# Chunked attention and a snake MLP: PSUM tiles in three shared slots, first loads issued together, V rows in four DMAs

## The chip, the cores and the metric

The kernel runs on one core of one Trainium2 chip. The metric is the device time of one execution in microseconds (us). The kernel before has three timed runs: 314.2, 314.21 and 312.73 us, median 314.2.

## What is computed

Four batches of eight heads with 768 positions of 64 values go through attention in chunks of 32 queries; each chunk sees its own 32 keys, 16 before, 8 after, and 8 memory keys of its head. The result, 3072 rows of 512, goes through a two-layer MLP with a snake activation.

```python
# per chunk c (32 queries), all batches and heads
k_full = concat([mem_k, k[c_start-16 : c_end+8]]); v_full = the same of mem_v, v
a = softmax(0.125 * q_c @ k_full.T)
x[c] = a @ v_full                     # x as (3072, 512)
# MLP
h = x @ w_in                          # 512 -> 2048
g = h + sin(alpha * h)**2 / alpha
out = g @ w_out                       # 2048 -> 512, float32
```

## The kernel before, in words

The program is written in the order in which each engine executes it; nothing reorders it. Each engine runs its own list from front to back, and waits in that list for the others.

**Loads.** Every load but one small one is issued by POOL: q and k of batch 0 in pairs of heads (L93), the memory keys and values (L145, L148), V of a batch in 16 DMAs (`load_v`, L116 and L120, two for each of eight blocks), the first-layer weights in eight DMAs (L181), the second-layer weights in four (L187), q and k of later batches in one DMA each (L106). POOL also copies the memory values into the V tiles (`put_memv`, L127) and the memory keys into the transposed keys (`put_memk`, L134).

**Attention of a batch.** For a pair of heads, VectorE copies k or q side by side (`pair_up`, tile `pr`, L195), TensorE transposes it (`t_k` L203, `t_q` L218), and ScalarE and VectorE bring the transpose into `kTi` and `qz` (L204, L210, L219, L223). Then `burst` goes over eight blocks of 96 queries: scores on TensorE (`qk_exp`, tile `sc`, L233), three exponentials on ScalarE (L247), and some steps later (the lag) the product with V (`pv`, tile `ot`, L261), the division by the row sum on VectorE (L264, L265) and a transpose into `xT` (L275, L278).

**First layer of a batch** (`l1`, 16 tiles `ft` of 128 of the 2048 columns): eight matmuls into `hT` (L301), a sine on ScalarE into `u` (L308), its square on ScalarE (L313) or VectorE (L311), and on VectorE the sum into `gT` (L314), which reads `hT` a second time and so frees its slot.

**Second layer** (`l2`): 96 matmuls of 512 columns (L327), 16 for each of six row groups; then the group is copied out of PSUM (L335 on VectorE, L337 on ScalarE in turn) and stored. They are handed out piecemeal as a filler: some in each step of the next batch's burst (`shares`), two behind each tile of the next first layer, the rest in one piece behind that.

**PSUM.** The pool `big` holds two slots of two 512-wide float halves, used by `sc` and `hT`; `opp` holds one slot for `o`; `atp` holds three small slots for transposes and `ot`. A tile waits until the readers of the slot's last tile are done.

**Order of the whole:** transposes of batch 0, burst 0, first layer 0 (with the transposes of batch 1 between its tiles, each behind the `l1` of its tile), burst 1 with second layer 0 as filler, first layer 1, and so on; the second layer of batch 3 ends the program.

## Time and profile before

| | |
|---|---|
| median of three timed runs | 314.2 us |
| profiled execution | 310.93 us, span 309.2 us |
| TensorE (PE) busy | 228.8 us, 74% of the span |
| VectorE (DVE) busy | 169.6 us, 55% |
| ScalarE (ACT) busy | 169.9 us, 55% |
| GpSimd (POOL) busy | 92.5 us, 30% |
| granted TensorE clock, mean | 0.961 |

How to read it: the span runs from the first to the last instruction of the profiled execution; its time is 1.7 us longer. "Busy" adds up an engine's instructions; matmul durations include the pipeline's length, so back-to-back matmuls overlap in it. In the rows that follow, the number before "us" or "ns" is what one instruction or one group took, and what stands behind an arrow is what ended the idle time before it. The stages lie, by the first rows of each in the timeline, at 0 to 43 us (loads, transposes, burst 0), 43 to 92.4 (first layer 0), 92.4 to 119.5 (burst 1), 119.5 to 159.9 (first layer 1), 159.9 to 181.3 (burst 2), 181.3 to 221.7 (first layer 2 and the rest of second layer 1), 221.7 to 244.1 (burst 3), 244.1 to 279.6 (first layer 3), 279.6 to 309.2 (the rest of second layer 2, all of second layer 3).

### The profile page before, as it was taken

Reading aid. Unit: us, or ns where it says so; the run is one execution under the profiler, and the core shown is the slowest. Engines: PE = TensorE matmul, PEld = TensorE weight load, DVE = VectorE, ACT = ScalarE, POOL = GpSimd, SP = SyncE. Lnnn points to the kernel's source line nnn. Section 1 sums busy time; section 2 is a strip of 40 time slices with the busy share of each in tenths; the row PEclk is TensorE's granted clock in tenths of the full one; section 3 lists DMA queues with packets and bytes.
Section 4 is the critical chain, followed back from the end, with each engine's and each line's share of the span. In section 5 each row is a group of like instructions: output and inputs, shape, how many; then the busy total and the mean of one; then the engine's idle time right before and its main releaser. Section 6 shows DMA issues by size and latency. Waiting matters only on the chain.

```text
span 309.2 us, 4313 instructions
## 1 busy us (share of the span) xinstructions
PE 228.8 (74%) x1604; PEld 130.5 (42%) x1604; DVE 169.6 (55%) x358; ACT 169.9 (55%) x256; POOL 92.5 (30%) x163
## 2 busy tenths in 40 slices
PE   1443783566739987888859978998789878887994
PEld 1331641333524553445435534545355444443441
DVE  6441653298870573677766646777566365554000
ACT  2435525277666505778885637798566367761000
POOL 8629985127967900000164900000000000000000
PEclk9999959699986999999989999999999999999999
DMA  8904999999499710000199900000101000001111
GB/s 100 113 1 29 91 144 199 205 205 101 30 145 144 106 37 34 2 34 0 9 182 146 97 34 2 35 0 2 68 19 51 36 0 34 0 3 69 68 68 69
DMA packets 54165, 20.97 MB, mean 68 GB/s; under 512 B 36736, under 2 KB 51072, under 8 KB 54144
## 3 DMA queue, kind: packets, MB, share of 16 engines
q0 software_dynamic: 48624, 14.40, 44.1%
q1 hardware_dynamic: 5520, 6.30, 5.8%
q8 instruction: 12, 0.20, 0.3%
q14 instruction: 9, 0.07, 0.1%
HBM read 28.78 MB, written 6.29 MB: 113 GB/s over the span
## 4 chain that ended last, share of the span: by engine, by line
PE 43%; DVE 21%; ACT 18%; POOL 7%; issue 5%; DMA 4%; DVEq 0%; ACTq 0%
PE o L327 22%; PE hT L301 15%; ACT u L308 8%; DVE gT L314 8%; ACT s L313 5%; DMA k_bf<-in_k_dram 4%; DVE s L311 4%; PE sc L233 2%; DVE qz L223 2%; DVE o_sb L335 2%; POOL w_in_sb L181 2%; POOL vw L120 2%; PE tk L203 2%; PE ot L261 2%; ACT o_sb L337 2%
## 5 line engine op out<-in xcount | busy, mean ns | idle before, releaser
L301 PE MATMUL hT<-xT,w_in_sb 128*128 128x384 bf16 x512 | 95.4, 332 | 24.2 <-DVE gT L314 22.8
L327 PE MATMUL o<-w_out_sb,gT 128*128 128x512 bf16 x384 | 102.6, 387 | 10.7 <-DVE o_sb L335 6.8
L314 DVE SCALAR_TENSOR_TENSOR gT<-s,inv_alpha,hT 128x768 bf16<-128x768 f32 x64 | 64.8, 1013 | 44.0 <-ACT s L313 39.8
L308 ACT ACTIVATE u<-hT,alpha_sb 128x768 f32<-128x768 f32 x64 | 57.7, 901 | 50.2 <-PE hT L301 49.9
L301 PEld LDWEIGHTS <-w_in_sb 128*128 128x128 bf16 x512 | 50.5, 99 | 68.3 <-issue 36.6
L247 ACT ACTIVATE pt<-sc,biasm 128x256 bf16<-128x256 f32 x96 | 37.9, 477 | 29.4 <-PE sc L233 29.4
L327 PEld LDWEIGHTS <-gT 128*128 128x128 bf16 x384 | 35.4, 99 | 39.7 <-issue 15.1
L313 ACT ACTIVATE s<-u 128x768 f32<-128x768 f32 x44 | 37.1, 843 | 1.4
L265 DVE TENSOR_TENSOR x_blk<-ot,rinv 96x256 bf16<-96x256 f32 x64 | 26.9, 421 | 2.2
L264 DVE RECIPROCAL rinv<-ot 96x4 f32<-96x4 f32 x64 | 11.1, 173 | 29.9 <-PE ot L261 29.9
L120 POOL DMA_DIRECT2D vw<-in_v_dram x32 | 23.3, 728 | 13.6 <-DMA q_bf<-in_q_dram 9.0
L337 ACT COPY o_sb<-o 128x512 f32<-128x512 f32 x12 | 7.0, 583 | 34.8 <-PE o L327 34.8
L233 PE MATMUL sc<-qz,kTi 128*128 128x192 bf16 x128 | 18.9, 283 | 8.9 <-DVE qz L223 6.0
L203 PE MATMUL tk<-ident,pr 128*128 128x128 bf16 x96 | 9.6, 248 | 21.3 <-DVE pr L195 21.3
L116 POOL DMA_DIRECT2D vw<-in_v_dram x32 | 22.0, 687 | 7.9 <-DMA w_out_sb<-in_moe_w_out_dram 4.2
L311 DVE TENSOR_TENSOR s<-u 128x768 f32<-128x768 f32 x20 | 19.2, 958 | 6.3 <-ACT u L308 6.0
L261 PE MATMUL ot<-vw,pt 128*128 128x65 bf16 x256 | 15.7, 203 | 9.1 <-DMA vw<-in_v_dram 3.9
L335 DVE COPY o_sb<-o 128x512 f32<-128x512 f32 x12 | 8.2, 687 | 25.8 <-PE o L327 25.8
L204 ACT COPY kTi<-tk 128x672 bf16<-128x672 bf16 x16 | 11.3, 707 | 18.2 <-PE tk L203 18.2
L261 PEld LDWEIGHTS <-pt 128*128 128x128 bf16 x256 | 13.1, 103 | 18.5 <-issue 4.0
L127 POOL COPY vw<-memv_st 8x512 bf16<-8x512 bf16 x32 | 18.9, 635 | 0.1
L233 PEld LDWEIGHTS <-kTi 128*128 128x128 bf16 x128 | 12.4, 111 | 12.6 <-issue 8.4
(43 smaller groups left out, 146.8 us busy)
## 6 DMA issues: line engine op xcount, KB each, us to landing
out_dram<-o_sb SPq DMA_DIRECT2D x24, 256.0 KB, 2.0
k_bf<-in_k_dram POOLq DMA_DIRECT2D x3, 768.0 KB, 8.6
q_bf<-in_q_dram POOLq DMA_DIRECT2D x3, 768.0 KB, 9.5
w_in_sb<-in_moe_w_in_dram POOLq DMA_DIRECT2D x8, 256.0 KB, 8.0
w_out_sb<-in_moe_w_out_dram POOLq DMA_DIRECT2D x4, 512.0 KB, 19.1
vw<-in_v_dram POOLq DMA_DIRECT2D x28, 64.0 KB, 3.5
vw<-in_v_dram POOLq DMA_DIRECT2D x28, 56.0 KB, 3.4
k_bf<-in_k_dram POOLq DMA_DIRECT2D x4, 192.0 KB, 4.0
```

The costliest lines, as they stand in the source:

```text
L116: nc.gpsimd.dma_start(vw[r0:64, :, j, 0:D], v[b, :, lo + r0:lo + 64, :].rearrange("h p d -> p h d"))
L120: nc.gpsimd.dma_start(vw[72:72 + n, :, j, 0:D], v[b, :, QW * j + 48:QW * j + 48 + n, :].rearrange("h p d -> p h d"),)
L233: nc.tensor.matmul(sc[:, hp // 2, 192 * (hp % 2):192 * (hp % 2) + 192].rearrange("p (e c) -> p e c", e=2), kTi[:, hp, 104 * j:104 * j + P] ...
L247: nc.scalar.activation(pt[:, 0:H * QW].rearrange("p (g e c) -> p g e c", g=2, e=4)[:, :, :, 32 * m:32 * m + 32], sc[:, :, 0:4 * QW].rearra ...
L261: nc.tensor.matmul(ot[:, e, :], pt[:, QW * h:QW * h + P], vws[b % 2][:, h, j, 0:D + 1])
L265: nc.vector.tensor_tensor(out=x_blk[:, 4 * g:4 * g + 4, :], in0=ot[0:QW, :, 0:D], in1=rinv[:, 4 * g:4 * g + 4].unsqueeze(2).to_broadcast([ ...
L301: nc.tensor.matmul(hT[:, hf, 0:HALF], w_in_sb[:, kt, P * ft:P * ft + P], xT[:, kt, HALF * hf:HALF * hf + HALF], start=(kt == 0), stop=(kt ...
L308: nc.scalar.activation(u[:], hT[:, :, 0:HALF], ACTF.Sin, scale=alpha_sb[:, ft:ft + 1])
L311: nc.vector.tensor_tensor(out=s2[:], in0=u[:], in1=u[:], op=ALU.mult)
L313: nc.scalar.activation(s2[:], u[:], ACTF.Square)
L314: nc.vector.scalar_tensor_tensor(out=gT[:, ft, :].rearrange("p (e c) -> p e c", e=2), in0=s2[:], scalar=inv_alpha[:, ft:ft + 1], in1=hT[:, ...
L327: nc.tensor.matmul(o[:], gT[:, ft, P * s:P * s + P], w_out_sb[:, ft, :], start=(ft == 0), stop=(ft == FT - 1),)
```

## The change

- `big` gets three slots, `atp` one. `ot` becomes one tile for all eight heads in `big`, with one reciprocal and one multiply in place of two each. The transposes of q and k take their slots in turn from `opp`, `big` and `atp` in batch 0, from two of them in the first layer of batch 0, and from `atp` after that.
- At the start, POOL issues all four pairs of q and k, the memory loads and V of blocks 0 and 1 before it builds the mask (`biasm`), then the rest of V, w_in, q and k of batch 1, w_out. V of batches 1 to 3 is loaded by four DMAs each (`load_v_all`).
- `put_memv` and `put_memk` become one VectorE copy each.
- The transposes of the next batch stand ahead of the `l1` of their tile instead of behind it, in batch 0 at tiles 8 to 15, in the others at 1, 3, 5, 7, 9, 11, 13 and 14. The pair copy for a transpose is made one transpose ahead.
- Burst 1 has lag 7 in place of 4, and shares that add up to more than 96: second layer 0 is used up in it, and first layer 1 has no filler. The last second layer alternates over three slots.

```diff
-    big = ctx.enter_context(tc.tile_pool(name="big", bufs=2, space=bass.MemoryType.PSUM))
+    big = ctx.enter_context(tc.tile_pool(name="big", bufs=3, space=bass.MemoryType.PSUM))
...
-    atp = ctx.enter_context(tc.tile_pool(name="atp", bufs=3, space=bass.MemoryType.PSUM))
+    atp = ctx.enter_context(tc.tile_pool(name="atp", bufs=1, space=bass.MemoryType.PSUM))
...
+    def load_v_all(b):
+        vw = vws[b % 2].rearrange("p h j c -> p (h j) c")
+        vf = v[b].rearrange("h s d -> (h s) d")
+        n = H * NJ
+        nc.gpsimd.dma_start(
+            vw[16:64, :, 0:D],
+            vf.rearrange("(n p) d -> p n d", p=QW)[0:48])
+        nc.gpsimd.dma_start(
+            vw[72:120, :, 0:D],
+            vf.rearrange("(n p) d -> p n d", p=QW)[48:96])
+        nc.gpsimd.dma_start(
+            vw[0:16, 1:n, 0:D],
+            vf.rearrange("(n p) d -> p n d", p=QW)[80:96, 0:n - 1])
+        nc.gpsimd.dma_start(
+            vw[120:128, 0:n - 1, 0:D],
+            vf.rearrange("(n p) d -> p n d", p=QW)[0:8, 1:n])
...
     def put_memv(b):
-        for h in range(H):
-            nc.gpsimd.tensor_copy(
-                vws[b % 2][64:72, h, :, 0:D],
-                memv_st[64:72, b, h, :].unsqueeze(1).to_broadcast([NM, NJ, D]),
-            )
+        nc.vector.tensor_copy(
+            vws[b % 2][64:72, :, :, 0:D],
+            memv_st[64:72, b].unsqueeze(2).to_broadcast([NM, H, NJ, D]),
+        )
...
     load_qk_pair(0, 0, *kq)
     masks.make_identity(nc, ident[:])
-    load_qk_pair(0, 1, *kq)
+    for hp in range(1, HP):
+        load_qk_pair(0, hp, *kq)
     for b in range(B):
         nc.gpsimd.dma_start(memk_bf[NM * b:NM * b + NM], mem_k[b].rearrange("h n d -> n h d"))
-    load_qk_pair(0, 2, *kq)
-    load_qk_pair(0, 3, *kq)
     nc.gpsimd.dma_start(memv_st[64:72].rearrange("n b h d -> n (b h) d"),
                         mem_v.rearrange("b h n d -> n (b h) d"))
+    load_v(0, 0)
+    load_v(0, 1)
     nc.gpsimd.memset(biasm[:], NEG)
...
-        for g in range(2):
-            ot = atp.tile([P, 4, D + 1], F32, name="ot", tag="at")
...
+        ot = big.tile([P, 2, 512], F32, name="ot", tag="big")
...
-            if last and s % 2 == 1:
-                o = atp.tile([P, d_model], F32, name="o2", tag="at")
+            if last and s % 3 == 1:
+                o = atp.tile([P, d_model], F32, name="o_a", tag="at")
+            elif last and s % 3 == 2:
+                o = big.tile([P, d_model], F32, name="o_b", tag="big")
...
+    prs = [pair_up(kq[n % 2], n // 2) for n in range(2)]
+    for n in range(2 * HP):
+        (t_k if n % 2 == 0 else t_q)(prs[n], n // 2)
+        if n + 2 < 2 * HP:
+            prs.append(pair_up(kq[n % 2], (n + 2) // 2))
...
     put_memk(0)
-    for j in range(NJ):
+    put_memv(0)
+    put_memv(1)
+    for j in range(2, NJ):
         load_v(0, j)
-        if j == 0:
-            put_memv(0)
...
-    for j in range(NJ):
-        load_v(1, j)
-    put_memv(1)
+    load_v_all(1)
...
+        state["pools"] = 2 if i == 0 else 1
+        at_ft = {8 + n: n for n in range(8)} if i == 0 else {
+            1: 0, 3: 1, 5: 2, 7: 3, 9: 4, 11: 5, 13: 6, 14: 7}
         for ft in range(FT):
             dve_sq = (ft % 2 == 1) if i == 0 else (ft % 4 == 3)
+            pc = None if last else at_ft.get(ft)
+            if pc is not None:
+                if pc == 0:
+                    prs = [pair_up(kq_next[0], 0)]
+                if pc < 7:
+                    prs.append(pair_up(kq_next[(pc + 1) % 2], (pc + 1) // 2))
+                (t_k if pc % 2 == 0 else t_q)(prs[pc], pc // 2)
             l1(i, ft, xT, gT, dve_sq)
-            if not last:
-                pc = {2: 0, 4: 1, 6: 2, 8: 3, 10: 4, 12: 5, 14: 6, 15: 7}.get(ft)
...
-            shares = (0, 5, 5, 6, 6, 6, 6, 6, 6, 6, 6, 6, 6)
-            xT = burst(i + 1, stream, shares, 4 if i == 0 else 1)
+            if i == 0:
+                xT = burst(i + 1, stream, (4, 8, 8, 8, 8, 8, 8, 8) + (6,) * 9, 7)
+            else:
+                xT = burst(i + 1, stream, (0, 5, 5, 6, 6, 6, 6, 6, 6, 6), 1)
             if i + 2 < B:
-                for j in range(NJ):
-                    load_v(i + 2, j)
+                load_v_all(i + 2)
                 put_memv(i + 2)
```

Two places show what moves. On POOL, at the start, before (`vw_88` is the V tile of batch 0, `memk_bf`, `memv_st` the memory rows, `biasm` the mask):

```order
L148 DMA memv_st<-in_mem_v_dram 8x32x64
L150 MEMSET biasm 128x5
L160 AFFINE_SELECT biasm<-biasm 128x1 x13
L134 COPY kTi<-memkT 128x8x8 x4
L116 DMA vw_88<-in_v_dram 48x8x64
L120 DMA vw_88<-in_v_dram 56x8x64
L127 COPY vw_88<-memv_st 8x8x64 x8
L116 DMA vw_88<-in_v_dram 64x8x64
```

and on POOL at the start now:

```order
L93 DMA k_bf<-in_k_dram 128x2x384
L93 DMA q_bf<-in_q_dram 128x2x384
L166 DMA memk_bf<-in_mem_k_dram 8x8x64 x4
L167 DMA memv_st<-in_mem_v_dram 8x32x64
L116 DMA vw_88<-in_v_dram 48x8x64
L120 DMA vw_88<-in_v_dram 56x8x64
L116 DMA vw_88<-in_v_dram 64x8x64
```

The V loads have moved ahead of the mask, and no copy of POOL that waits for another engine stands among them any more; the mask comes one DMA later, then the other twelve V loads and w_in.

On VectorE, the first tiles of first layer 1 before (`gT` is the sum that frees an `hT` slot, `pr` a pair copy, `s_...` the squares):

```order
L314 SCALAR_TENSOR_TENSOR gT<-s_1270,inv_alpha,hT 128x768
L314 SCALAR_TENSOR_TENSOR gT<-s_1284,inv_alpha,hT 128x768
L195 COPY pr<-k_bf 128x2x6x64
L314 SCALAR_TENSOR_TENSOR gT<-s_1302,inv_alpha,hT 128x768
L195 COPY pr<-q_bf 128x2x6x64
L210 COPY kTi<-tk 128x48 x2
L311 TENSOR_TENSOR s_1330<-u 128x768
```

and on VectorE at the same place now:

```order
L340 SCALAR_TENSOR_TENSOR gT<-s_1204,inv_alpha,hT 128x768
L212 COPY pr<-k_bf 128x2x6x64
L212 COPY pr<-q_bf 128x2x6x64
L238 COPY kTi<-tt_a 128x48 x2
L340 SCALAR_TENSOR_TENSOR gT<-s_1232,inv_alpha,hT 128x768
L340 SCALAR_TENSOR_TENSOR gT<-s_1246,inv_alpha,hT 128x768
```

The first pair copies stand behind the first `gT` instead of the second, with the copies of the transposed keys (`kTi`) ahead of the second `gT`; from there on a pair copy stands one transpose ahead of its use.

## The prediction

> **What bounds the kernel now.** I read the page first, then busy time by stage, then the chain of waits inside a stage.

> ```profile
> span 309.2 us, 4313 instructions
> PE 228.8 (74%) x1604; PEld 130.5 (42%) x1604; DVE 169.6 (55%) x358; ACT 169.9 (55%) x256; POOL 92.5 (30%) x163
> ```

> No engine is full, so time is lost where engines wait in turn. The stages (columns: stretch and its length, then busy us of PE, PEld, DVE, ACT, POOL, the granted clock, DMA):

> ```profile
> 0.00:43.00 43.00, 19.24 (x180) 14.47 (x180) 22.64 (x81) 17.60 (x34) 33.47 (x69) 0.96 0.79 73
> 43.00:92.40 49.40, 28.50 (x181) 16.77 (x180) 31.97 (x45) 27.64 (x33) 27.67 (x42) 0.88 1.17 148
> 92.40:119.50 27.10, 24.45 (x196) 13.82 (x196) 12.49 (x42) 11.89 (x27) 13.20 (x24) 0.90 0.80 94
> 119.50:159.90 40.40, 30.81 (x204) 17.79 (x204) 27.49 (x41) 31.17 (x38) 3.77 (x5) 0.99 0.20 34
> 159.90:181.30 21.40, 19.07 (x178) 11.47 (x178) 12.40 (x42) 11.30 (x26) 14.41 (x26) 0.94 1.07 118
> 181.30:221.70 40.40, 35.12 (x222) 19.40 (x222) 27.49 (x41) 30.01 (x38) 0.00 (x0) 1.00 0.04 14
> 221.70:244.10 22.40, 18.14 (x181) 10.88 (x179) 12.43 (x42) 13.16 (x28) 0.00 (x0) 1.00 0.13 48
> 244.10:279.60 35.50, 29.02 (x155) 15.06 (x155) 18.63 (x21) 24.75 (x29) 0.00 (x0) 1.00 0.02 9
> 279.60:309.20 29.60, 24.49 (x112) 10.86 (x111) 4.03 (x5) 2.34 (x4) 0.00 (x0) 1.00 0.19 71
> ```

> In the first stage POOL is the busiest (33.5 of 43 us). The four first layers (rows 2, 4, 6, 8) take 166 us together, with PE, DVE and ACT each 50 to 87% busy. What binds them is one loop, read from the chain in first layer 3:

> ```profile
> 248.38 1.48 PE hT L301 x8
> 249.88 0.91 ACT u L308
> 250.81 0.85 ACT s L313
> 251.69 1.02 DVE gT L314
> 252.75 1.47 PE hT L301 x8
> ```

> An `hT` slot is held 4.37 us, and there are two: 2.19 us a tile. The last stage is PE alone and stays as it is.

> **Start (43 us).**

> ```profile
> 14.00 0.82 PE L203 MATMUL tk<-ident,pr 128*128 128x128 bf16 x6 [2.27 <-DVE pr L195]
> 17.73 0.82 PE L203 MATMUL tk<-ident,pr 128*128 128x128 bf16 x6 [2.27 <-DVE pr L195]
> 21.34 0.76 POOL L134 COPY kTi<-memkT 128x64 bf16<-128x64 bf16 x4 [7.67 <-DVE memkT L350]
> 23.49 4.51 POOL L127 COPY vw<-memv_st 8x512 bf16<-8x512 bf16 x8
> 37.67 5.99 POOL L181 DMA_DIRECT2D w_in_sb<-in_moe_w_in_dram  x8
> L120 POOL DMA_DIRECT2D vw<-in_v_dram x32 | 23.3, 728 | 13.6 <-DMA q_bf<-in_q_dram 9.0
> L160 POOL TENSOR_SCALAR_AFFINE_SELECT biasm<-biasm 128x1 f32<-128x1 f32 x13 | 2.2, 186 | 0.6
> ```

> A pair of heads takes 3.73 us (14.00 to 17.73), because the next pair copy stands behind the 0.96 us copy into `qz`. It now stands ahead of it: about 2.9, three pairs, 2.5 us less. POOL began with V only after the memory keys (22.1 us), then spent 4.5 on the memory values, so w_in was first issued at 37.7. Now nothing waits there. At 0.7 us a DMA (the V row's, rounded down, since V's other DMAs and the small ones are shorter), eight pair loads, five memory loads and four V loads take 11.9, the identity matrix 0.5, the mask 2.2 and some gaps, the other twelve V loads 8.4: from a start at 1.3 that makes about 25.2. So the loads from w_in on come 12.5 us earlier. Burst 0 can begin at 19.2, and is then bound by ACT and DVE.

> ```profile
> L308 ACT ACTIVATE u<-hT,alpha_sb 128x768 f32<-128x768 f32 x64 | 57.7, 901 | 50.2 <-PE hT L301 49.9
> L314 DVE SCALAR_TENSOR_TENSOR gT<-s,inv_alpha,hT 128x768 bf16<-128x768 f32 x64 | 64.8, 1013 | 44.0 <-ACT s L313 39.8
> L313 ACT ACTIVATE s<-u 128x768 f32<-128x768 f32 x44 | 37.1, 843 | 1.4
> L311 DVE TENSOR_TENSOR s<-u 128x768 f32<-128x768 f32 x20 | 19.2, 958 | 6.3 <-ACT u L308 6.0
> L264 DVE RECIPROCAL rinv<-ot 96x4 f32<-96x4 f32 x64 | 11.1, 173 | 29.9 <-PE ot L261 29.9
> L265 DVE TENSOR_TENSOR x_blk<-ot,rinv 96x256 bf16<-96x256 f32 x64 | 26.9, 421 | 2.2
> L278 DVE COPY xT<-xtp 128x384 bf16<-128x384 bf16 x32 | 11.1, 347 | 6.2 <-PE xtp L275 6.2
> L223 DVE COPY qz<-tq 64x768 bf16<-64x768 bf16 x16 | 15.4, 961 | 1.9 <-ACT qz L219 1.6
> L219 ACT COPY qz<-tq 64x768 bf16<-64x768 bf16 x16 | 12.5, 782 | 0.7 <-PE tq L218 0.5
> L195 DVE COPY pr<-k_bf 128x768 bf16<-128x768 bf16 x16 | 6.2, 386 | 6.2 <-DMA k_bf<-in_k_dram 6.1
> ```

> A block costs DVE 0.2 + 0.72 + 0.35 = 1.27 us; the merged reciprocal and multiply lie between one and two of the old (0.59 and 1.19), I take 0.92. The merged memory copies are new on DVE: 4096 elements at the `pr` row's rate are 2.1 us, at the `xT` row's 3.7; both tiles are plain bf16 copies like `pr`, so I take 2.0 each; behind the first exponentials they could cost nothing, and the `xT` rate bounds them at 3.7. They end at 23.3, eight blocks add 10.2: first layer 0 starts at 33.5 where it started at 43. **Gain 9.5.**

> **First layer 0 (49.4 us).**

> ```profile
> 56.88 0.36 DVE L195 COPY pr<-k_bf 128x768 bf16<-128x768 bf16 x1 [6.09 <-DMA k_bf<-in_k_dram]
> 60.73 0.36 DVE L195 COPY pr<-q_bf 128x768 bf16<-128x768 bf16 x1 [2.56 <-DMA q_bf<-in_q_dram]
> ```

> 8.7 us went on waiting for k and q of batch 1, with all later sums, and so the `hT` slots, queued behind on DVE. They landed 19.2 and 23.1 us behind the first w_in issue; from 25.2 that is 44.4 and 48.3. Tiles 0 to 7 have no transposes: with three slots the loop allows 1.46 us a tile, DVE needs (2 x 1.01 + 0.96) / 2 = 1.5, so they end at 33.5 + 3.3 + 12.2 = 49.0, just behind q. From tile 8 on the transpose of tile ft waits for a pair copy behind `gT` of tile ft-2, so that the third slot is of little use: two tiles take 1.47 + 0.91 + 0.85 + 1.02 + 0.39 and a transpose of 0.4, with hand-offs 5.1 us; DVE's own work is 5.0. So: two pair copies 0.8, transpose 0.4, then 1.47 + 0.91 + 0.85 + 1.02 end `gT` of tile 8 at 54.4; three pairs 15.3, the last tile 3.5, the keys' copy 0.3 make 73.5, a stage of 40.0. **Gain 9.4.**

> **Burst 1 and first layer 1 (67.5 us).** Burst 1 takes over the 26 matmuls of second layer 0 that the first layer had.

> ```profile
> 283.89 20.89 PE o L327 x96
> 181.35 2.60 PE L301 MATMUL hT<-xT,w_in_sb 128*128 128x384 bf16 x15 [0.28 <-DVE xT L278]
> PE o L327 <- DVE o_sb L335: 6.8, 9, 1.4
> ```

> 26 x 0.218 = 5.7 and one more wait of 0.75 for the single `o` slot: 27.1 becomes 33.5. **Loss 6.4.** V in four DMAs is not shown before: 120 x 64 rows of 128 bytes are 0.98 MB, at the first stage's 73 GB/s 13 us. They queue behind w_out, whose 2.1 MB at the second stage's 148 GB/s land 14 us behind q, at 62.5; V then lands at 76. The first product with V stands at step 7 of burst 1, some 15 us into it, at 88: twice the time for V is still covered, and a faster V earns nothing, so I take zero. In first layer 1, tile 1 now waits on PE for the pair copy behind the first `gT`: 4.2 + 0.4 + 0.4 = 5.0 us before the second `hT`. From there ACT is the bound: 11 tiles at 0.90 + 0.84 = 19.1, four sines alone 3.6, eight copies at 0.78 = 6.2, together 28.9; the last square and sum on DVE 2.0, the keys 0.4: 36.3 for 40.4. **Gain 4.1.**

> **The rest.** Bursts 2 and 3 keep their fillers and their lag; `ot` takes the slot of scores whose exponentials it needs anyway: 0.2 less each for a shorter division. First layer 2: PE now needs 16 x 1.39 + 8 x 0.4 + 44 x 0.218 + three waits of 0.75 and the 3.5 of the first tile, 40.8 us for 40.4: **no gain**, its old waits were covered by the filler. First layer 3 has no transposes: 1.39 + 0.44 = 1.83 us a tile on PE against 2.19; fifteen are 27.4, with the first tile, two waits for `o` and the end 30.5 for 35.5. **Gain 5.0.**

> The sum: 9.5 + 9.4 - 6.4 + 4.1 + 0.4 + 0 + 5.0 = 22.0 us, a span of 287.2; the profiled execution took 310.93, 1.7 above its span, so 288.9. The three timed runs' median, 314.2, lies 1.05% above that execution: **292 us**. Half a per cent, 1.6 us, is about what a measurement here can tell from no change.

> **The clock.**

> ```profile
> 92.41 0.96 PE L233 MATMUL sc<-qz,kTi 128*128 128x192 bf16 x5 [3.51 <-DVE qz L223]
> 92.40:95.00 2.60, 2.59 (x10) 1.45 (x10) 0.00 (x0) 2.23 (x6) 1.69 (x3) 0.50 1.35 202
> ```

> Burst 1 begins behind 3.5 us in which PE waited, at a granted clock of 0.50 (column after POOL). I keep such a start, about 2.5 us, in bursts 1 and 2, since PE waits there as long as before. [...]

> [...]

> **Rivals.** (1) The third slot brings nothing, because slots are freed by instructions in line behind others on DVE: first layers 1 and 3 gain 0.6 together, the start and the removed wait remain: 13.5 us, 300. For it: in two of four first layers PE's order ties `hT` to pair copies. Against: first layer 3 has none. 0.18. (2) The clock stays up: 287. 0.07. [...] 0.1. (4) The bubbles close: burst 1 at PE's work alone (27.5), the first tiles of first layers 1 and 2 without theirs: 11 us more, 281. 0.1. (5) Slower: the transposes, now ahead of the `hT` matmuls on PE, are each held for a pair copy just behind the `gT` before, so that each such tile goes through 5.0 us alone instead of 2.2: 2.8 us each. It would have to hold for 22 / 2.8 = 8 more of the 24 to eat the gain; for all, 350 us. Against it: the order on DVE, where pair copies stand one transpose ahead but for the first. 0.05.

> **How the numbers follow.** The forecast has 0.5; its own range is 285 to 299, from the memory copies' bounds (3 us), the landing of q (4) and burst 1 (4). The range takes in rivals 1 to 4 up to 279 and 304, and leaves out the slow one and the tails. All cases but 5 are faster by over 0.5%: faster 0.94, same 0.02, slower 0.04.

> **What would show it.** Right: w_in issued by 27 us; first `hT` by 35; no wait of VectorE for k or q over 2 us; burst 1 at 73 and 33 long; first layer 1 with ACT busy over 85% behind its second tile; first layer 3 near 30 us. [...]

## The result, and the profile after

The changed kernel takes 298.43 us (median of four runs, 294.53 to 300.54) where the kernel before, run beside it, takes 313.47: a ratio of 0.946, with a 95% interval of 0.932 to 0.959. The forecast was 292, with a range of 279 to 304. The time is 6.4 us above the forecast, so what follows asks where those microseconds went. One thing is needed to read the numbers: every ratio here leaves out executions more than 1.5% above the shortest of their kernel, of these four 300.54 us (the profiled one, mean granted clock 0.949) and 299.49, where the shortest had 0.977.

The page of the changed kernel, its span and its first row:

```profile
span 298.8 us, 4113 instructions
PE 229.0 (77%) x1583; PEld 132.2 (44%) x1604; DVE 166.9 (56%) x302; ACT 169.1 (57%) x256; POOL 51.7 (17%) x79
```

POOL went from 92.5 to 51.7 us; the others do the same work in 10 us less. By stage, the same columns as before the change (stretch and length, busy us of PE, PEld, DVE, ACT, POOL, then the granted clock, the DMA share and GB/s):

```profile
0.00:33.86 33.86, 17.97 (x181) 14.39 (x181) 23.76 (x68) 17.74 (x34) 29.77 (x56) 0.98 0.99 92
33.86:77.00 43.14, 29.31 (x178) 16.23 (x177) 30.99 (x46) 27.83 (x33) 15.65 (x18) 0.89 1.90 172
77.00:112.08 35.08, 29.29 (x222) 16.41 (x227) 11.44 (x28) 12.57 (x28) 0.32 (x1) 0.95 1.22 86
112.08:150.08 38.00, 25.05 (x175) 14.64 (x175) 28.05 (x42) 30.32 (x37) 6.00 (x6) 0.98 0.28 39
150.08:172.97 22.89, 20.31 (x178) 12.45 (x183) 10.74 (x27) 11.30 (x26) 0.00 (x0) 0.88 1.51 84
172.97:216.06 43.09, 36.22 (x215) 20.23 (x219) 28.64 (x43) 29.59 (x37) 0.00 (x0) 0.92 0.04 13
216.06:240.25 24.19, 19.67 (x179) 11.88 (x181) 10.80 (x26) 13.17 (x28) 0.00 (x0) 0.93 0.12 44
240.25:271.57 31.32, 28.77 (x161) 16.03 (x164) 20.39 (x21) 24.23 (x29) 0.00 (x0) 1.00 0.05 18
271.57:298.80 27.23, 22.41 (x101) 9.95 (x102) 2.08 (x4) 2.34 (x4) 0.00 (x0) 1.00 0.18 67
```

The table sets them beside the stages of before and the forecast's terms. A first layer runs here from its first `hT` (within 0.6 us) to the scores of the next burst that stand behind the last wait for its keys and queries, the last one to its last `gT` (so first layer 3 before is 37.48 us here, and the forecast's gain of 5.0 is taken off that).

| stage | before | forecast | after |
|---|---|---|---|
| start and burst 0 | 43.07 | 33.5 | 33.86 |
| first layer 0 | 49.34 | 40.0 | 43.14 |
| burst 1 | 27.14 | 33.5 | 35.08 |
| first layer 1 | 40.39 | 36.3 | 38.00 |
| burst 2 | 21.41 | 21.2 | 22.89 |
| first layer 2 | 40.14 | 40.1 | 43.09 |
| burst 3 | 22.68 | 22.5 | 24.19 |
| first layer 3 | 37.48 | 32.5 | 31.32 |
| rest | 27.55 | 27.6 | 27.23 |

The start came out as forecast, and the last first layer better. Every stage between them is 1.6 to 3.1 us too long, and in each of those the clock column (the granted clock of TensorE, 1 for full and 0.50 for half) stands below 1.

At the start, on POOL and VectorE (time, length, engine, line):

```profile
18.92 0.69 POOL L116 DMA_DIRECT2D vw<-in_v_dram  x1
19.60 1.68 POOL L120 DMA_DIRECT2D vw<-in_v_dram  x1
19.79 2.52 DVE L144 COPY vw<-memv_st 8x4096 bf16<-8x4096 bf16 x2
21.28 1.31 POOL L116 DMA_DIRECT2D vw<-in_v_dram  x1
28.80 5.97 POOL L198 DMA_DIRECT2D w_in_sb<-in_moe_w_in_dram  x8
```

The memory copies took 1.26 us each, and the two V loads issued beside them 1.68 and 1.31 us where their neighbours take 0.7: 1.6 us more on POOL. The two loads end at 21.28 and 22.59, each just behind a copy (21.05 and 22.31); what stretched them no trace shows. w_in was issued at 28.8, not 25.2, and q of batch 1 landed near 52 instead of 48.

In first layer 0 the clock, in stretches of 2 us, and the wait of PE at tile 8:

```profile
32.00:34.00 2.00, 0.88 (x12) 0.77 (x10) 1.45 (x5) 0.15 (x1) 2.00 (x4) 0.67 1.34 179
34.00:36.00 2.00, 1.90 (x7) 0.71 (x5) 0.36 (x1) 0.00 (x0) 1.62 (x3) 0.50 1.28 164
36.00:38.00 2.00, 2.00 (x8) 0.97 (x7) 0.00 (x0) 1.07 (x2) 1.68 (x3) 0.50 1.39 181
38.00:40.00 2.00, 2.00 (x9) 0.98 (x8) 1.01 (x1) 1.21 (x2) 1.00 (x2) 0.62 1.44 192
```

```profile
51.96 0.35 DVE L212 COPY pr<-k_bf 128x768 bf16<-128x768 bf16 x1
52.23 0.35 DVE L212 COPY pr<-q_bf 128x768 bf16<-128x768 bf16 x1
52.37 0.51 PE L231 MATMUL tt_o<-ident,pr 128*128 128x128 bf16 x6 [3.88 <-DVE pr L212]
```

The first tiles ran at half clock, so eight tiles were done at 52.0 instead of 49.0, and q's late landing doesn't show: the pair copies have no wait of their own. The 8.7 us that VectorE spent waiting for k and q are gone.

In first layers 1 and 2 the transposes at tile 1 wait for a pair copy behind the first `gT`, the second time at 177.45:

```profile
177.45 0.82 PE L231 MATMUL tt_a<-ident,pr 128*128 128x128 bf16 x6 [3.19 <-DVE pr L212]
```

The clock is at half from 176 to 183 us, by the same columns as the stages:

```profile
177.00:179.00 2.00, 1.55 (x9) 1.06 (x10) 0.66 (x3) 0.69 (x1) 0.00 (x0) 0.50 0.00 0
179.00:181.00 2.00, 2.00 (x7) 0.88 (x6) 0.32 (x2) 0.16 (x2) 0.00 (x0) 0.50 0.00 0
181.00:183.00 2.00, 2.00 (x8) 0.90 (x7) 0.32 (x1) 1.61 (x2) 0.00 (x0) 0.53 0.03 8
```

Read in steps of half a microsecond, the clock lay below 0.95 in six stretches of the changed kernel's profile: at 32.5 to 39.5, 53 to 57, 77 to 80.5, 148.5 to 156, 176 to 183 and 220 to 224 us. Added up as (1 - clock) times length, each of them lost 1.7 or 3.4 us of clock, 15.3 together; before the change it was 11.9 in four. So there were two theories of the missing 6 to 12 us: the half clock behind the new waits, or the waits themselves and q's landing.

### The profile page after: what moved, and what is told of

Same layout as the page of the kernel before. It is cut to its first block, busy times and chain, and to the rows that moved or that the text cites. A ratio compares the mean times of both kernels' runs of the same rounds, so it can differ in the third digit from the quotient of the medians.

```text
span 298.8 us, 4113 instructions
## 1 busy us (share of the span) xinstructions
PE 229.0 (77%) x1583; PEld 132.2 (44%) x1604; DVE 166.9 (56%) x302; ACT 169.1 (57%) x256; POOL 51.7 (17%) x79
## 4 chain that ended last, share of the span: by engine, by line
PE 55%; DVE 20%; ACT 17%; issue 6%; DVEq 0%; ACTq 0%
PE o L355 22%; PE hT L327 17%; ACT u L334 7%; DVE gT L340 5%; ACT s L339 5%; PE sc L259 4%; DVE qz L251 3%; DVE s L337 3%; PE ot L286 3%; PE o_a L355 2%; PE o_b L355 2%; ACT pt L273 2%; DVE o_sb L363 2%; DVE pr L212 2%; PE xtp L301 2%
## 5 line engine op out<-in xcount | busy, mean ns | idle before, releaser
L327 PE MATMUL hT<-xT,w_in_sb 128*128 128x384 bf16 x512 | 98.7, 340 | 2.4 <-DVE gT L340 1.5
L355 PE MATMUL o<-w_out_sb,gT 128*128 128x512 bf16 x301 | 84.5, 392 | 14.6 <-DVE o_sb L363 8.5
L340 DVE SCALAR_TENSOR_TENSOR gT<-s,inv_alpha,hT 128x768 bf16<-128x768 f32 x64 | 64.4, 1013 | 39.0 <-ACT s L339 36.7
L327 PEld LDWEIGHTS <-w_in_sb 128*128 128x128 bf16 x512 | 50.8, 102 | 39.6 <-issue 10.8
L273 ACT ACTIVATE pt<-sc,biasm 128x256 bf16<-128x256 f32 x96 | 38.0, 478 | 30.0 <-PE sc L259 29.9
L339 ACT ACTIVATE s<-u 128x768 f32<-128x768 f32 x44 | 37.1, 843 | 1.4
L290 DVE RECIPROCAL rinv<-ot 96x8 f32<-96x8 f32 x32 | 6.5, 202 | 29.8 <-PE ot L286 29.7
L291 DVE TENSOR_TENSOR x_blk<-ot,rinv 96x512 bf16<-96x512 f32 x32 | 22.0, 686 | 1.1
L365 ACT COPY o_sb<-o 128x512 f32<-128x512 f32 x10 | 5.8, 583 | 27.4 <-PE o L355 25.6
L337 DVE TENSOR_TENSOR s<-u 128x768 f32<-128x768 f32 x20 | 19.1, 955 | 2.2 <-ACT u L334 2.0
L363 DVE COPY o_sb<-o 128x512 f32<-128x512 f32 x10 | 6.9, 687 | 22.2 <-PE o L355 21.9
L231 PEld LDWEIGHTS <-pr 128*128 128x128 bf16 x96 | 7.1, 110 | 27.0 <-DVE pr L212 23.1
L106 POOL DMA_DIRECT2D k_bf<-in_k_dram x3 | 2.7, 897 | 77.7 <-DVE pr L212 77.3
L304 DVE COPY xT<-xtp 128x384 bf16<-128x384 bf16 x32 | 11.1, 347 | 6.4 <-PE xtp L301 6.4
L246 PEld LDWEIGHTS <-pr 128*128 128x128 bf16 x96 | 7.1, 112 | 16.0 <-DVE pr L212 10.2
L246 PE MATMUL tt_a<-ident,pr 128*128 128x128 bf16 x78 | 7.2, 234 | 9.1 <-DVE pr L212 6.0
```

What stands on the lines that cost most here:

```text
L246: nc.tensor.transpose(t[:, r, :], qb[:, r].rearrange("p e d -> p (e d)"), ident[:])
L273: nc.scalar.activation(pt[:, 0:H * QW].rearrange("p (g e c) -> p g e c", g=2, e=4)[:, :, :, 32 * m:32 * m + 32], sc[:, :, 0:4 * QW].rearra ...
L291: nc.vector.tensor_tensor(out=x_blk[:].rearrange("p (g e) d -> p g e d", g=2), in0=otv[0:QW, :, :, 0:D], in1=rv.unsqueeze(3).to_broadcast( ...
L327: nc.tensor.matmul(hT[:, hf, 0:HALF], w_in_sb[:, kt, P * ft:P * ft + P], xT[:, kt, HALF * hf:HALF * hf + HALF], start=(kt == 0), stop=(kt ...
L337: nc.vector.tensor_tensor(out=s2[:], in0=u[:], in1=u[:], op=ALU.mult)
L339: nc.scalar.activation(s2[:], u[:], ACTF.Square)
```

## The experiments

Twelve runs of eleven kernels; times are medians beside the kernel before on the same chip, and "the changed kernel" is 298.43.

### Two slots instead of three (two_slots)

```diff
-    big = ctx.enter_context(tc.tile_pool(name="big", bufs=3, space=bass.MemoryType.PSUM))
+    big = ctx.enter_context(tc.tile_pool(name="big", bufs=2, space=bass.MemoryType.PSUM))
```

> The changed kernel with two slots in the pool big in place of three; two banks of PSUM stay unused, all else is as changed. Prediction's theory (the third slot lets a first layer run at the pace of PE, ACT or DVE instead of the 4.37 us hold): first layer 3 goes from 29.4 back to 35 us, first layer 0 gets some 4 to 5 us longer (tiles 0 to 7 at 2.19 instead of 1.5 us), first layers 1 and 2 by 1 to 3 us, the bursts by 0 to 3 us each where values and scores share two slots: 12 to 18 us above the changed kernel's 298, so 310 to 316. Rival 1 (slots are freed by instructions that stand in line on VectorE anyway): under 2 us in all, first layer 3 under 31.

320.6 us, ratio to before 1.026 (1.019 to 1.033): slower than the kernel before the change, and 4.6 us beyond the range expected. First layer 3:

```profile
256.96:294.45 37.49, 31.08 (x165) 16.04 (x165) 20.57 (x21) 24.75 (x29) 0.00 (x0) 1.00 0.04 15
```

The waits of PE for a slot of `hT` over the whole run (total us, times, longest), here and then in the changed kernel:

```profile
PE hT L327 <- DVE gT L340: 24.4, 29, 1.6
```

```profile
PE hT L327 <- DVE gT L340: 1.5, 4, 0.5
```

First layer 3 is back at 37.5, the value of before, and the others lost 4.2, 6.6 and 2.6 us (the second of them partly by half clock). Burst 0 lost 4.3 as well, more than expected; `ot` takes slots of `big` too since the change, so values and scores now share two. Rival 1 falls: without the third slot the rest of the change costs more than it brings. How much of that is the `hT` loop and how much the shared `ot`, only first layer 3 shows, with 6.2 us.

### POOL's start as before (old_start)

```diff
-    for hp in range(1, HP):
-        load_qk_pair(0, hp, *kq)
+    load_qk_pair(0, 1, *kq)
     for b in range(B):
         nc.gpsimd.dma_start(memk_bf[NM * b:NM * b + NM], mem_k[b].rearrange("h n d -> n h d"))
+    load_qk_pair(0, 2, *kq)
+    load_qk_pair(0, 3, *kq)
...
-    load_v(0, 0)
-    load_v(0, 1)
...
-    put_memk(0)
-    put_memv(0)
-    put_memv(1)
-    for j in range(2, NJ):
+    for hp in range(HP):
+        nc.gpsimd.tensor_copy(
...
+    for j in range(NJ):
         load_v(0, j)
+        if j == 0:
+            pool_memv(0)
...
+    pool_memv(1)
```

> The changed kernel with POOL's start as before: head pairs 2 and 3 behind the memory keys, the mask ahead of V, the memory copies of batches 0 and 1 as 64x8 and 128x64 pieces on POOL; the pipelined pair copies of the start stay. Theory (POOL's order sets the start and the landing of k and q): w_in first issued at 35 to 37 instead of 28.8, first hT at 39 to 41 instead of 33.9, k and q of batch 1 land at 55 to 59, of which the eight tiles without transposes hide most, so first layer 0 is 0 to 4 us longer: 6 to 9 us above the changed kernel, 304 to 307. Rival (the pipelined pair copies alone made the start's gain): within 2 us of the changed kernel. [...]

305.51 us, ratio 0.978 (0.973 to 0.982): 7.1 above the changed kernel. Its first two stages:

```profile
0.00:41.85 41.85, 18.98 (x180) 14.16 (x181) 21.60 (x66) 17.96 (x34) 34.29 (x69) 0.97 0.82 76
41.85:84.72 42.87, 28.50 (x177) 16.14 (x177) 30.87 (x46) 27.73 (x33) 19.48 (x25) 0.91 1.80 172
```

On POOL, the first w_in issue and a later issue that waited until q of batch 1 had landed:

```profile
36.11 5.99 POOL L204 DMA_DIRECT2D w_in_sb<-in_moe_w_in_dram  x8
59.38 0.83 POOL L139 DMA_DIRECT2D vw<-in_v_dram  x1 [3.06 <-DMA q_bf<-in_q_dram]
```

The start is 8.0 us longer, about as expected, so POOL's order is what made it short: the first part of w_in landed at 41.81 us here, and the first `hT` began at 41.85. First layer 0 is not longer (42.87 against 43.14), though q came about 7 us later in it: with the transposes at tiles 8 to 15, eight tiles cover the load either way. So the gain of first layer 0 is not that of the earlier loads. The third slot has a part in it (4.2 us longer without); the moved transposes are what is left, and no run moves them alone.

### Burst 1 with the old lag and shares (lag4)

```diff
-                xT = burst(i + 1, stream, (4, 8, 8, 8, 8, 8, 8, 8) + (6,) * 9, 7)
+                xT = burst(i + 1, stream, (0, 5, 5, 6, 6, 6, 6, 6, 6, 6, 6, 6, 6), 4)
```

> The changed kernel with burst 1's old lag of 4 and old shares: 26 matmuls of second layer 0 go back from burst 1 into first layer 1. Theory of the granted clock (PE goes to half clock behind waits of over 3 us, which the filler closes): burst 1 near 29 us instead of 35.1, first layer 1 near 39 to 40 instead of 38.0 with its 3.2 us wait at the second tile and the 3.7 us at its end shortened by filler, and burst 2 starts warm, 21.4 instead of 22.9: 3 to 7 us below the changed kernel, 291 to 295. Rival (the two moves cancel, as the prediction's 6.4 lost and 4.1 gained nearly do): 0 to 2 us below. Second rival (V in four DMAs lands too late for a lag of 4): PE waits for DMA vw in burst 1 and the time rises.

291.0 us, ratio 0.930 (0.926 to 0.934): 7.4 below the changed kernel, and outside the range of its four runs. Burst 1 and first layers 1 and 2, and under them 4 us of first layer 2 behind its wait:

```profile
76.20:102.64 26.44, 23.75 (x200) 13.59 (x200) 10.83 (x27) 11.88 (x27) 0.33 (x1) 0.94 1.71 94
102.64:144.42 41.78, 31.59 (x202) 17.91 (x201) 28.73 (x43) 30.99 (x38) 5.99 (x6) 0.96 0.28 47
166.69:207.14 40.45, 33.79 (x220) 19.21 (x219) 28.65 (x43) 29.53 (x37) 0.00 (x0) 1.00 0.04 14
171.00:173.00 2.00, 1.82 (x15) 1.23 (x16) 0.71 (x4) 0.72 (x1) 0.00 (x0) 1.00 0.00 0
173.00:175.00 2.00, 2.00 (x13) 1.09 (x12) 0.17 (x1) 1.95 (x3) 0.00 (x0) 1.00 0.03 8
```

The wait itself, at tile 1 of first layer 2:

```profile
171.18 0.51 PE L231 MATMUL tt_a<-ident,pr 128*128 128x128 bf16 x6 [3.19 <-DVE pr L212]
```

Burst 1 is 8.6 us shorter and first layer 1 3.8 longer, a net 4.9 in favour of the old lag. First layer 2 teaches more: nothing in it was edited, it has the same wait of 3.19 us, but the clock stayed at 1.00, and it took 40.45 where the changed kernel's profile has 43.09. So one such wait, followed or not followed by half clock, differs by 2.6 us. The expectation had the right time but not all of its reasons: burst 2 did not start warm (22.3 us, half clock from 145.6), and first layer 1 took 2 us more than expected. Its 3 us for a wait that brings half clock was the author's estimate: the 3.19 us here brought none.

### The first pair copies earlier (early_pr)

```diff
+        if 0 < i and not last:
+            prs = [pair_up(kq_next[n], 0) for n in range(2)]
         for ft in range(FT):
...
-                if pc == 0:
+                if i == 0 and pc == 0:
                     prs = [pair_up(kq_next[0], 0)]
-                if pc < 7:
+                if pc < 7 and (i == 0 or pc > 0):
```

> The changed kernel with the first two pair copies of batches 2 and 3 made ahead of the first tile's gT instead of behind it, so that the transposes in front of the second hT of first layers 1 and 2 find them ready. Theory (those two waits of 3.19 us lie on the path, and the half clock from 173 to 182 follows from the second): each first layer gets 2.5 to 3 us shorter, first layer 2 another 1.5 to 2.5 by the clock: 6 to 8 us below the changed kernel, 290 to 292. Rival (the wait only moves on, to the single slot of the transposes and ACT, which is near full behind tile 1): under 2 us in all, first layer 1 over 37 us.

289.29 us, ratio 0.926 (0.922 to 0.929): 9.1 below the changed kernel. First layers 1 and 2 and burst 3:

```profile
110.92:146.22 35.30, 25.08 (x175) 14.64 (x175) 28.05 (x42) 30.11 (x37) 5.99 (x6) 1.00 0.31 43
168.39:206.05 37.66, 33.84 (x219) 19.22 (x219) 28.64 (x43) 29.31 (x37) 0.00 (x0) 1.00 0.04 15
206.05:228.60 22.55, 18.35 (x182) 11.09 (x181) 10.71 (x26) 13.17 (x28) 0.00 (x0) 1.00 0.13 47
```

What is left of the wait in first layer 2:

```profile
170.04 0.51 PE L231 MATMUL tt_a<-ident,pr 128*128 128x128 bf16 x6 [0.35 <-DVE pr L212]
```

First layer 2 at full clock takes 37.66 with the copies ahead and 40.45 (the kernel above) with them behind: the wait itself is worth 2.8 us, and the half clock that may follow it another 2.6. First layer 1 gained 2.7. Burst 3 is 1.6 shorter though nothing in it changed: its first product waits 1.93 us for ScalarE in both kernels, here at 1.00, there followed by half clock.

### The changed kernel again (after_again)

> The changed kernel once more, unaltered, for a second profiled execution. In the first one the granted clock was below 0.95 in six stretches (32.5 to 39.5, 53 to 57, 77 to 80.5, 148.5 to 156, 176 to 183 and 220 to 224 us), each about 3.5 or 7 us long. Theory (whether a wait of PE is followed by such a stretch hangs on when it falls, not on its length alone): the same waits with other stretches, first layer 2 near 40.4 where none follows its 3.19 us wait, times spread over 294 to 301 us. Rival (the schedule fixes them): the same six stretches, every stage within 0.5 us of the first profile's.

299.54 us (295.78 to 300.73), ratio 0.953 (0.946 to 0.961). First layers 1 and 2:

```profile
112.05:152.24 40.19, 27.47 (x175) 15.73 (x175) 28.03 (x42) 30.41 (x37) 5.99 (x6) 0.92 0.27 38
174.13:216.25 42.12, 35.47 (x219) 19.76 (x219) 28.64 (x43) 29.55 (x37) 0.00 (x0) 0.96 0.04 14
```

The same program, the same waits, but now half clock follows the wait of first layer 1 as well (115 to 122), and one stretch instead of two that of first layer 2 (179.5 to 183.5). First layer 1 is 2.2 us longer, first layer 2 1.0 shorter. Four of the seven stretches lie where they lay, two are half as long and one is new: neither theory held whole. Whether half clock follows differs from execution to execution (the last section shows what went with it), and the changed kernel's times go with it: 294.5 us at a mean clock of 0.977, 295.8 at 0.971, 300.5 and 300.7 at 0.949. First layer 2 near 40.4 was not seen here.

### Both edits (early_lag4)

> The changed kernel with both edits that helped: the first two pair copies of batches 2 and 3 ahead of the first gT, and burst 1's old lag of 4 and old shares. Theory (they act in different places): burst 1 near 26.5 us, first layer 1 at 38.5 to 39.5 (the 41.8 of the lag edit less the 2.8 of its wait), first layer 2 near 37.7, together 281 to 285 us. Rival (both remove the same waits, since filler closed part of them): 287 to 289, no better than the pair copies alone.

284.1 us, ratio 0.912 (0.906 to 0.918), burst 1 at 26.43, first layer 1 at 37.25, first layer 2 at 37.64. The gains add up, nearly: 14.3 below the changed kernel, against 7.4 and 9.1 alone. First layer 1 came out 1.2 us better than expected.

### k and q earlier (kq_first), and TensorE kept busy in its waits (warm_kq)

The first edit alone, then with added matmuls:

```diff
-    for c in range(8):
+    for c in range(4):
         load_w_in(c)
     kq_next = load_qk(1)
+    for c in range(4, 8):
+        load_w_in(c)
```

```diff
+    def idle_mm(n, pool, tag):
+        w = pool.tile([P, 512], F32, name="idle_out", tag=tag)
+        for _ in range(n):
+            nc.tensor.matmul(w[:], ident[:], idle_in[:])
+            yield
...
-    xT = burst(0, empty, (), 2)
+    xT = burst(0, Stream(idle_mm(12, opp, "o")), (0,) * 8 + (4, 4, 4), 2)
...
+            if (i == 0 and ft == 7) or (i in (1, 2) and ft == 0):
+                Stream(idle_mm(10, atp, "at")).take(11)
+            if i == 1 and ft == FT - 1:
+                Stream(idle_mm(12, opp, "o")).take(13)
```

> The changed kernel with k and q of batch 1 issued ahead of the last four w_in loads instead of behind them. The rival explanation of first layer 0 (43.1 us where 40.0 was forecast) is that q landed at 52 us, 4 us late, and held the pair copies: then first layer 0 is 2 to 4 us shorter. The theory (gT of tile 7 itself ended at 52.0, because the first tiles ran at half clock): first layer 0 within 1 us of the changed kernel's in a profile with as much half clock there, the total within 1.5 us of the changed kernel's.

> The kernel with k and q of batch 1 ahead of the last four w_in loads, and with 54 added matmuls of 512 columns whose result nobody reads, put where TensorE waits: 12 in the last three steps of burst 0, 10 ahead of the transposes at tile 8 of first layer 0 and at tile 1 of first layers 1 and 2, 12 behind the last tile of first layer 1. The waits stay as long; only TensorE is busy in them. Clock theory: no stretch below 0.95 at 33 to 40, 53 to 57, behind the second tiles of first layers 1 and 2 and at the start of burst 2; first layer 0 at 38 to 40.5 us, burst 2 at 21.2 to 21.6, first layer 2 at 40 to 40.5, 4 to 8 us below the kernel with the k and q edit alone. Rival (the waits cost, not the clock): within 1 us of that kernel, or above it by the added 11.8 us of TensorE's work where it is on the path.

The edit of the loads alone: 298.31 us (294.42 to 302.82), ratio 0.949 (0.942 to 0.956), the same as the changed kernel. q landed at 46.9 us instead of 52.1, and first layer 0 took 42.1 us, 1.1 less, with 6.8 us of half clock in it instead of 9.1. The rival explanation by q's landing falls. With the added matmuls: 291.63 us (290.97 to 292.12), ratio 0.936 (0.931 to 0.940), and the spread is gone. First layer 0, burst 2, first layer 2 and burst 3:

```profile
34.78:74.31 39.53, 27.15 (x186) 15.48 (x185) 30.37 (x45) 27.73 (x33) 14.07 (x16) 1.00 1.94 179
147.39:168.33 20.94, 18.21 (x181) 11.08 (x182) 10.74 (x27) 11.30 (x26) 0.00 (x0) 1.00 2.03 93
168.33:208.77 40.44, 35.94 (x229) 20.20 (x229) 28.63 (x43) 29.52 (x37) 0.00 (x0) 1.00 0.04 14
208.77:231.32 22.55, 18.36 (x183) 11.09 (x182) 10.72 (x26) 13.17 (x28) 0.00 (x0) 1.00 0.13 48
```

54 matmuls more, 11.8 us of work at 0.218 each, made the kernel 6.7 us faster. The waits are where they were (first layer 2 takes 40.44, as in the kernel with the old lag, where the clock stayed up by itself); only the clock differs: one stretch is left, at the start of burst 1, which had no added matmul. This settles the cause of the microseconds missing in the changed kernel: with the clock held up, the stages lie within 1.7 us of the forecast's.

### Transposes in two slots (two_tr)

```diff
-        state["pools"] = 2 if i == 0 else 1
+        state["pools"] = 2 if i <= 1 else 1
```

(on the kernel with added matmuls)

> The kernel with added matmuls (warm_kq), and in first layer 1 the transposes take their slots in turn from two pools instead of one. The forecast of first layer 1 (36.3 us) held ACT to be its bound behind the second tile; with the clock at 1.00 it took 38.0. Theory (the single slot of the transposes keeps PE and then ACT waiting, 5.4 us of PE waits for qz and kTi in it): 36 to 37 us in first layer 1. Rival (ACT or VectorE bound it anyway): 37.5 to 38.

294.12 us, ratio 0.940 (0.935 to 0.945), 2.5 above the kernel it is compared with, with two more half-clock stretches in its profile. First layer 1:

```profile
110.36:149.62 39.26, 30.94 (x195) 17.41 (x196) 27.77 (x42) 30.03 (x37) 5.99 (x6) 0.96 0.34 44
```

One half-clock stretch (141 to 144.5) lies in it. Taking off at most its 1.7 us leaves 37.6: the single slot is not what holds first layer 1. The waits for `qz` and `kTi` went, others (for `gT` 2.6 us, for `pr` 4.5) took their place. The theory falls.

### V in sixteen DMAs (v16)

```diff
-    load_v_all(1)
+    for j in range(NJ):
+        load_v(1, j)
...
-                load_v_all(i + 2)
+                for j in range(NJ):
+                    load_v(i + 2, j)
```

(on the kernel with added matmuls)

> The kernel with added matmuls (warm_kq), and V of batches 1 to 3 in sixteen DMAs a batch as before the change. The prediction's zero (V lands long before its first product either way): within 1 us of warm_kq, 290.6 to 292.6. Rival (four DMAs spare POOL or the DMA engines something on the path): 1 to 4 us more. Second rival (four DMAs land later and were paid for in bursts 2 and 3, with their lag of 1): 0.5 to 2 us less.

292.07 us (291.83 to 292.29), ratio 0.935 (0.930 to 0.940), 0.4 from the kernel it is compared with, while POOL was busy 72.1 us instead of 51.8. The four DMAs spare POOL 20 us, and nothing waits for POOL there: the prediction's zero holds.

### All that helped (best, best_again)

The kernel with both edits and k and q earlier, and added matmuls at four waits: the end of burst 0, tile 8 of first layer 0, and the ends of first layers 0 and 1. The lines that follow show where the places of the added matmuls differ from those of warm_kq.

```diff
-            if (i == 0 and ft == 7) or (i in (1, 2) and ft == 0):
+            if i == 0 and ft == 7:
                 Stream(idle_mm(10, atp, "at")).take(11)
-            if i == 1 and ft == FT - 1:
+            if i <= 1 and ft == FT - 1:
```

> All edits that helped in one kernel: the first two pair copies of batches 2 and 3 ahead of the first gT, burst 1 with its old lag of 4 and old shares, k and q of batch 1 ahead of the last four w_in loads, and added matmuls that nobody reads in four waits of TensorE (12 at the end of burst 0, 10 at tile 8 of first layer 0, 12 each behind the last tile of first layers 0 and 1). Theory (waits and clock add up): stages of 34.5, 39.5, 25, 37.3, 21, 37.6, 22.6 us and 58.6 for the rest, clock 1.00 throughout, 276 to 280 us. Rival (the added matmuls delay real work, or the pair copies and the filler remove the same time twice): 281 to 285, no better than the two edits without added matmuls.

> The kernel with all helpful edits once more, unaltered, for a profile at the usual clock: in the first one the granted clock was 0.75 from 28 us to the end (325.03 us), while five other executions took 278.3 to 280.35. Theory (the 0.75 belongs to that one execution): stages of 34.5, 39.5, 25, 37.3, 21, 37.6, 22.6 us and 58.6 for the rest, mean clock over 0.98, 276 to 281 us. Rival (the added matmuls bring the 0.75 about): again at least one execution near 325.

The first time 279.78 us (median of six, 278.3 to 280.35 and one execution of 325.03), ratio 0.895 (0.891 to 0.898); the second time 278.58 (278.08 to 279.54), ratio 0.889 (0.883 to 0.896). It beats the kernel before by 11% and the changed kernel by 6.7%. From its second profile, burst 1 with a warm start and burst 3, where the one remaining stretch lies:

```profile
74.45:99.21 24.76, 21.91 (x197) 12.96 (x201) 10.83 (x27) 11.65 (x27) 0.32 (x1) 1.00 1.64 113
195.05:219.26 24.21, 19.80 (x180) 11.84 (x181) 10.76 (x26) 13.14 (x28) 0.00 (x0) 0.93 0.12 45
```

The stages stand at 34.9, 39.5, 24.8, 37.3, 20.9, 37.7, 24.2 and 58.5 us against 34.5, 39.5, 25, 37.3, 21, 37.6, 22.6 and 58.6 expected; only burst 3 missed, by its half clock.

## Why the prediction was right, and where it was off

**Direction, range and mechanism held.** Without the third slot the change loses 22 us, without the new start 7; both were named as the sources. Of the signs named, the first `hT` (33.86), the waits for k and q, ScalarE at 87% in first layer 1 and first layer 3 (31.3) came; w_in issued by 27 and burst 1 at 73 and 33 long did not (28.8, 77.0 and 35.1).

**Some of the closeness is luck.** The sum gave 288.9 us for an execution like the profiled one, and 292 only because the three timed runs lay 1.05% above that one; nothing in the change makes those 3 us. Against the measured median the sum was 9.5 us short, by stages 11.6 in the profiled execution.

**The step that was mis-sized is the clock:** the prediction kept a cold start of 2.5 us in bursts 1 and 2 and took the rest of the kernel as warm. In the profile of the changed kernel, 15.3 us of clock went in six stretches, in first layers 0 and 2 and burst 3 too. Held up by added matmuls, the same schedule took 291.6 us, and its stages, 34.78, 39.53, 35.08, 38.00, 20.94, 40.44, 22.55, 31.32 and 27.26, are 2.7 us above the forecast's sum of 287.2.

**Start, 9.5 forecast, 9.2 measured.** Errors cancelled. The memory copies took 1.26 us each, not 2.0, but VectorE, taken as the bound of burst 0, then waited 2.6 us for TensorE in it. w_in came 3.6 us later than worked out, because POOL waits on earlier DMAs (1.4 and 0.7 us), the mask took 2.8, and two V loads were stretched (1.68 and 1.31 us where 0.7 was counted); its first part landed at 33.81, just ahead of the first `hT`, so a shorter burst alone would have brought nothing.

**First layer 0, 9.4 forecast, 6.2 measured.** The sum is right at full clock (39.5 against 40.0), its reason only in part. The prediction had the earlier loads end the wait for k and q; with the old start the wait did not come back. The moved transposes hid it, by their place; no run tests them alone.

**Burst 1 and first layer 1, a net loss of 2.3 forecast, 5.6 measured.** The longer lag costs burst 1 8.6 us, not 6.4: beside the 5.7 of the 26 matmuls, five waits for `o` of 0.78 to 0.91 us (4.2) stand in place of four of 0.45 to 0.78 (2.4), and PE waits another 1.0 for `xT` in the last steps, where only products are left. In first layer 1 ACT is busy for 28.3 of the 32.7 us behind the second tile (87%; here in the kernel of warm_kq, at full clock):

```profile
114.70:147.39 32.69, 25.51 (x173) 14.59 (x171) 25.29 (x38) 28.29 (x35) 6.00 (x6) 1.00 0.32 44
```

It is the busiest of the engines, as the forecast had it, but not without gaps: 32.7 us where 31.3 were worked out. That it is the bound isn't shown, since no run makes its work less. And taking the filler out of it brings 2 us, not 4: with the pair copies ahead it takes 37.25 us with filler and 35.30 without. The longer lag is a net loss of 5 to 7 us in time where 2.3 was forecast.

**First layer 2, "no gain", 3.0 lost.** At full clock it is 40.4, the old value. The prediction saw the wait at tile 1 of first layers 1 and 2 and put it into its sums as given; making two copies of a batch earlier removes it with the clock's share, 9 us in all.

**First layer 3, 5.0 forecast, 6.2 measured;** the loop runs at PE's pace as named, 1.73 us a tile by the starts of its rows where 1.83 was worked out.

**The rivals.** Rival 1 (the third slot brings nothing) is refuted by the run with two. Rival 5 (transposes held in every tile) shows only at tile 1 of first layers 1 and 2. Rival 2 (the clock stays up, which takes the 2.5 us kept in each of two bursts off the 292: 287) is what did not happen: the clock moved the other way, and held up by force it gives 291.6. The chances and the range also count rival 3, V loads held up beside the new memory copies, with 4 us at the start; no run shows those 4 us. What the runs showed in their place is two V loads of 1.68 and 1.31 us beside the copies, 1.6 us on POOL (with no such copy beside them, all sixteen V loads of batch 0 took 0.64 to 0.76 us in the kernel before and 0.63 to 0.74 with the old start); how much of that reached the path through w_in, no run shows. Rival 4 (the bubbles close, 281) didn't come of the change itself; the kernel with early copies and old lag closes most of them, at 284.

## What to carry to other kernels

A wait of TensorE had two prices here: its length (the 3.19 us in first layer 2 were worth 2.8), and a half-clock stretch that may follow (1.7 or 3.4 us of clock). Look for stretches of some 3.4 us in which waits leave TensorE less than half busy (below 41% half clock followed in every one from the first `hT` on), fill them with work that is due anyway, or move the one small copy that causes them, before adding buffers. When a change shifts filler between stages, cost the stage that receives it with its own waits, and the lag apart from the filler.

## What the runs showed of the hardware

```profile
172.64:176.06 3.42, 1.34 (x8) 0.58 (x6) 1.49 (x2) 1.73 (x2) 0.00 (x0) 1.00 0.06 22
176.06:179.47 3.41, 2.02 (x11) 1.33 (x12) 1.88 (x5) 0.73 (x2) 0.00 (x0) 0.50 0.00 0
```

```profile
166.07:169.49 3.42, 1.64 (x12) 0.69 (x9) 1.58 (x2) 1.43 (x2) 0.00 (x0) 1.00 0.14 53
169.49:172.90 3.41, 1.72 (x15) 1.21 (x16) 1.88 (x5) 1.03 (x2) 0.00 (x0) 1.00 0.00 0
```

TensorE is busy for 3.36 us of the two windows in both, but in the first kernel one window has only 1.34 of it (39%), and the next runs at half clock; in the second they have 1.64 and 1.72 (48 and 50%), and the clock stays. In 13 profiles (all but the one with 0.75 below), 909 windows from the first `hT` on began at full clock: all 43 in which PE was busy less than 41% were followed by half clock, none of the 853 with 46% or more, and 10 of the 13 between. Ahead of the first `hT`, 7 of 22 windows were followed too, at 49 to 67%, so there this share alone doesn't decide. Waits shorter than a window of 3.41 us were enough: 1.93 us in burst 3, 3.19 in first layer 2.

The clock column says nothing of the first microseconds, where the traces have no clock record (up to 29.3 us in the changed kernel): six transposes took 0.82 us at 177.45, at half clock, and 0.51 at 52.37, at full clock; the six at 14.00 in the kernel before, ahead of its first clock record, took 0.82 as well.

One execution of the best kernel in ten ran at a granted clock of 0.75 from 28 us to its end and took 325.03 us, a row from its middle:

```profile
200.00:204.00 4.00, 4.00 (x20) 2.13 (x19) 2.20 (x6) 3.19 (x5) 0.00 (x0) 0.75 0.00 0
```

It did not come again in the four later ones. Whether the added matmuls make it likelier stays open: one case in ten executions here, none in the other kernels' runs.
